# First tile's rows transposed at once, the second weight converted among the first products, the first expert's tiles taken as one, two, two, one

## The chip, the core and the metric

The kernel runs on one core of a Trainium2 chip. The metric is device microseconds (us) for one execution, from the first instruction to the end; the smaller the better. The core has five engines with queues of their own: TensorE (PE: products, and PEld: the loads of the stationary operand), VectorE (DVE), ScalarE (ACT), GpSimd (POOL) and SyncE (SP), which issues all DMAs here.

## The reference

Three stages stand one behind the other: attention with a block-causal mask (4 batches, 8 heads, 576 rows, 64 numbers a head), a layer of four experts, and a last layer with a softmax gate and a normalisation.

```python
scores = scale * np.matmul(q, k.transpose(0, 1, 3, 2))   # masked by blocks of 64
attn = softmax(scores); attn_out = np.matmul(attn, v)
x = attn_out.transpose(0, 2, 1, 3).reshape(B * S, H * D)  # 2304 x 512
p = domain_probs / (domain_probs.sum(-1, keepdims=True) + 1e-09)
for e in range(E):                                        # E = 4
    h = np.maximum(x @ w1[e], 0.0)                        # 512 -> 1024
    out += p[:, e:e + 1] * (h @ w2[e])                    # 1024 -> 512
# then: h = x @ w_in; solu = h * softmax(h); layer norm; @ w_out
```

## The kernel before

**Numbers as pairs.** A product of float32 values is made from three products of float16 pairs: a high part, and a low part that holds what the high part leaves. A weight is loaded in four parts as float32, its squares are summed on ACT (`square`, L127), a power-of-two scale is worked out (`scale`: L244, one product at L246, then DVE at L248, L131, L135 and L138), and each part is split (`split`: the high half on POOL at L257 or on ACT at L261, the low half on DVE at L264). For the first expert's two weights POOL makes the high halves. Queries and keys are prepared in the same manner (`parts`, L481 and L483, in most cases both on POOL), and so are values (`v_split`, L564 on POOL, L565 on DVE).

**Tiles and steps.** The 2304 rows are 18 tiles of 128. Tiles 0 and 1 hold the first 64 rows of two batches each; tiles 2 to 5 are the rest of the first batch. A tile takes several attention steps: two each for tiles 0 and 1, four for tiles 2, 3 and 4, eight for tile 5. So steps 0 to 3 are tiles 0 and 1, steps 4 to 7 tile 2 (scores 192 columns wide), 8 to 11 tile 3 (320 wide), 12 to 15 tile 4 (448 wide), and 16 onwards tile 5 (two halves of 288). A step has three parts: `step_a` makes scores (L600, L601, L604), `step_b` the exponentials (L639), their split (L643 on ACT, L644 on DVE) and a DMA transpose to `pT`, and `step_c` the products with the values (L673). When all steps of a tile are done, `finish` has three parts of its own: `rows` (L715) divides by the sums, `scale` squares the rows and works out a scale, `split` makes the pair (L726 on ACT, L727 on DVE) and transposes it by DMA to `xT`. From then on the experts can use the tile.

**Experts.** `emit_h` makes `h` of a run of k tiles: for each of 8 column blocks f of the first weight 12 products of 128*k columns (L306), and then one evacuation on ACT (L314) and one on DVE (L315) for every 3 // k column blocks. So a run of one tile takes the blocks as three, three and two; a run of two or three tiles takes one at a time. `emit_o` makes the second product of a tile, 24 products of 512 columns (L326). `h` lies in 8 buffers (`hp`); a run of two or three tiles uses all 8. The six tiles of the first part belong to expert 0 as six runs of one tile; all later phases have runs of three.

**The order.** The work up to step 3 is emitted from a string of letters (L958), one letter a piece: `a`, `b`, `c` are the three parts of the next step, `f` is the next of the three parts of `finish`, `W` the next piece of the first expert's first weight (its squares, scale and splits), `x` and `X` the same of its second weight (loads and pieces), `V` the next piece of the first batch's values (five squares, the scale, two splits), `N` the next keys and queries of tile 2, and `n, v, p, y, z, t, u` loads. Behind the string, what is left is emitted: for letters in a fixed order, then steps, then `finish`. All DMAs issued up to there keep their emitted order on SP (`InOrder`, L79).

Then a planner (L1009) emits the steps from 4 on and the expert units between them, by two clocks that it keeps itself. A unit waits until its last tile is `ready`. Pieces of weights come either from a list `bg` by step number, up to three behind a step, or as units among the expert units (`spread`, L978). In the kernel before, the rest of the first expert's second weight is in `bg` from step 2 on, and no expert unit is emitted before it is through (`len(bg) <= n1`, L1011).

The emitted order gives each instruction its rank. A scheduler then places instructions on each engine's queue, those that it thinks ready in the order of rank, so that ready work of a later rank can stand ahead of waiting work of an earlier one. Each engine runs its own queue in that order.

Of the kernel before, what the change touches and what calls it, by code (L numbers as in the profile page):

```python
# [58 lines left out]
def tile_kernel(  # L59
# [51 lines left out]
    psh = phs.enter_context(tc.tile_pool(name="psh", bufs=NPH, space=PSUM))  # L111
# [285 lines left out]
    def phase_units(j, runs, pool):  # L397

        e = j % E
        units = []  # L400
        for t0, k in runs:
            cost = 12 * (k * 128 / 2400 + 0.003)
            per = GT // k
            for f in range(0, KF, per):
                fs = range(f, min(f + per, KF))
                units.append((t0 + k - 1, lambda t=t0, k=k, fs=fs: emit_h(e, t, k, fs, pool), cost * len(fs)))
            for t in range(t0, t0 + k):
                units.append((
                    t, lambda t=t, o=(t - t0) * 128: out_unit(e, t, o, pool), 24 * 0.216,
                ))  # L410
        return units
# [474 lines left out]
    p1, q1 = next_w(gp, place_raw="w2")  # L886
# [44 lines left out]
    def token(c, left=0):  # L931

        for l in before.get(c, ""):
            while todo[l]:
                todo[l].pop(0)()
        if todo[c]:
            todo[c].pop(0)()
# [17 lines left out]

    ready = {}
    strict[0] = True
    for c in "naSyczZTPPnpwpWbcTZWzxufvWfWPpfzxSTfazSTPwTnbVbyWTapbnwabvvcVPNnVbnVPwxbNuXtPnztzu":  # L958
        if c == "f":
            at1.token_f()  # L960
        elif c in "abc":
            if c == "a" and at1.na < 20 or c == "b" and at1.nb < at1.na or c == "c" and at1.nc < at1.nb:
                getattr(at1, "token_" + c)()
        elif todo[c]:
            token(c)
# [10 lines left out]
    p1, q1 = todo["x"], todo["X"]  # L976

    def spread(units, *spans):  # L978

        todo = []  # L980
        for a, b, tasks in spans:
            todo += [(a + (b - a) * (k + 1) / len(tasks), fn) for k, fn in enumerate(tasks)]
        todo.sort(key=lambda x: x[0])
        res = []
        for j, u in enumerate(units):
            while todo and todo[0][0] <= j:
                res.append((None, todo.pop(0)[1], 0.0))
            res.append(u)
        return res + [(None, fn, 0.0) for _, fn in todo]


    p2, q2 = next_w()
    p3, q3 = next_w()
    bg = [(2, fn) for fn in p1 + q1]
    bg += [(14, fn) for fn in p2 + q2] + [(32, fn) for fn in p3]
    moe = phase_units(0, [(t, 1) for t in range(6)], psh)
    post = q3
    for j in range(1, 5):
        us = phase_units(j, GROUPS[j // E], psh)
# [5 lines left out]
    moe.reverse()  # L1005
    bg.reverse()
    tpe = tdv = 0.0
    n1 = len(p2 + q2 + p3)
    while at1.more:  # L1009
        t, u, cost = moe[-1] if moe else (-1, None, 0)  # L1010
        ok = t is None or t in ready and len(bg) <= n1  # L1011
        if not ok or tdv <= tpe + 2.0:
            at1.step()
            a, c = at1.cost()
            tdv, tpe = tdv + (a * 1.2 if at1.n < SLOW else PACE + c), tpe + c
            for _ in range(3):
                if bg and bg[-1][0] <= at1.n:
                    bg.pop()[1]()
        else:
            moe.pop()  # L1020
            u()
            tpe += cost
# [196 lines left out]
```

## Time and profile before

| what | value |
|---|---|
| median of 3 runs | 1137.04 us (1136.17 to 1137.23) |
| the profiled execution | 1137.2 us |
| its span, first to last instruction | 1135.4 us |
| TensorE products busy | 1072.7 us, 94% of the span |
| DVE, ACT, POOL busy | 712.2, 504.7, 181.6 us |
| mean granted TensorE clock | 0.991 of full speed |

The span lies 1.8 us under the execution's time. An engine is busy while an instruction of its own runs; products are pipelined, so a busy TensorE isn't one at its peak. The granted clock is the share of full speed (2.4 GHz) that TensorE had: 0.5 would be 1.2 GHz throughout.

### The profile page before, as it was taken

The numbers are of one execution on the slowest core, as the hardware profiler recorded it, in microseconds if no ns is written. First come the engines' busy times: TensorE is split into PE (matmuls) and PEld (weight loads), VectorE is DVE, ScalarE is ACT, GpSimd is POOL, SyncE is SP. The second block draws the span as 40 slices with busy tenths as digits, with TensorE's granted clock in tenths as the row PEclk, the third lists the DMA queues.
The fourth block names the chain that finished last, engine by engine and source line by source line (L and its number), as shares of the span: only waits on it lengthen the run. The fifth ranks groups of instructions, "written<-read, shape, count | busy, mean of one in ns | idle before, by whom it ended". The sixth has DMA issues, their size and how long they took to land.

```text
span 1135.4 us, 18547 instructions
## 1 busy us (share of the span) xinstructions
PE 1072.7 (94%) x7216; PEld 609.2 (54%) x7216; DVE 712.2 (63%) x1562; ACT 504.7 (44%) x1067; POOL 181.6 (16%) x176
## 2 busy tenths in 40 slices
PE   4579889899999999999999999999999999999998
PEld 4456766466556555655555555555555554444443
DVE  7988788557676876555313223232788646999883
ACT  5567676646656666562333213131324342333222
POOL 4975533224125310000000000000000000000000
PEclk9999999899999999999999999999999999999999
DMA  9768996738638747334121002020232111353343
GB/s 319 222 165 171 229 201 160 211 81 229 164 92 207 189 103 163 52 111 142 54 96 49 27 1 75 1 74 1 75 93 84 31 27 28 74 103 74 84 84 83
DMA packets 216056, 125.77 MB, mean 111 GB/s; under 512 B 183712, under 2 KB 185760, under 8 KB 215456
## 3 DMA queue, kind: packets, MB, share of 16 engines
q1 hardware_dynamic: 215968, 124.59, 42.7%
q8 instruction: 56, 0.92, 0.4%
q14 instruction: 32, 0.26, 0.1%
HBM read 73.18 MB, written 6.29 MB: 70 GB/s over the span
## 4 chain that ended last, share of the span: by engine, by line
PE 77%; DMA 8%; DVE 6%; POOL 4%; issue 2%; ACT 2%; SPq 1%; ACTq 0%; POOLq 0%; DVEq 0%
PE ops L326 29%; PE hps L306 27%; PE h L1070 8%; PE o L1133 8%; DMA pT<-hl 6%; PE pv L673 2%; DVE wt L264 1%; PE sps L600 1%; DMA stage<-in_w_dram 1%; DVE hl L644 1%; PE sps L601 1%; POOL wt L257 1%; POOL v L564 1%; ACT p L639 1%; POOL ks L483 1%
## 5 line engine op out<-in xcount | busy, mean ns | idle before, releaser
L306 PE MATMUL hps<-xT,wt 128*128 128x384 f16 (+1 forms) x2688 | 396.0, 305 | 3.5 <-DVE hch L315 3.1
L326 PE MATMUL ops<-wt,hch 128*128 128x512 f16 x1728 | 386.7, 381 | 2.5 <-DVE hch L315 1.3
L306 PEld LDWEIGHTS <-wt 128*128 128x128 f16 x2688 | 239.7, 99 | 138.4 <-issue 6.9
L326 PEld LDWEIGHTS <-hch 128*128 128x128 f16 x1728 | 167.4, 98 | 196.5 <-issue 6.0
L314 ACT ACTIVATE hch<-hps 128x384 f16<-128x384 f32 (+1 forms) x194 | 93.8, 485 | 232.1 <-PE hps L306 231.4
L315 DVE SCALAR_TENSOR_TENSOR hch<-hps,hch 128x384 f16<-128x384 f32 (+1 forms) x194 | 106.2, 550 | 131.1 <-ACT hch L314 130.7
L639 ACT ACTIVATE p<-sps,nm 128x320 f32<-128x320 f32 (+4 forms) x144 | 79.0, 552 | 80.8 <-DVE nm L610 46.6
L644 DVE TENSOR_TENSOR hl<-p,hl 128x320 f16<-128x320 f32 (+4 forms) x132 | 89.5, 692 | 33.7 <-ACT hl L643 33.3
L264 DVE SCALAR_TENSOR_TENSOR wt<-stage,ws,wt 128x1024 f16<-128x1024 f32 x72 | 97.4, 1377 | 12.8 <-ACT wt L261 11.5
L127 ACT ACTIVATE junk<-stage 128x1024 bf16<-128x1024 f32 x72 | 75.9, 1054 | 57.5 <-DMA stage<-in_w_dram 44.1
L350 DVE SCALAR_TENSOR_TENSOR acc<-ops,coef,acc 128x512 f32<-128x512 f32 x54 | 40.4, 748 | 90.8 <-PE ops L326 90.8
L1070 PE MATMUL h<-wt,x2T 128*128 128x512 f16 x432 | 95.5, 379 | 0.8 <-DVE acc L350 0.8
L1133 PE MATMUL o<-wt,lt 128*128 128x512 f16 x432 | 95.5, 379 | 0.0
L600 PE MATMUL sps<-ks,qhi 128*128 128x288 f32 (+3 forms) x160 | 66.0, 416 | 19.0 <-ACT p L639 8.4
L673 PE MATMUL pv<-v,pT 128*128 128x64 f16 x1392 | 56.2, 198 | 18.4 <-DMA pT<-hl 18.4
L261 ACT ACTIVATE wt<-stage,ws 128x1024 f16<-128x1024 f32 x64 | 70.4, 1141 | 4.6 <-DVE ws L138 4.6
L1070 PEld LDWEIGHTS <-x2T 128*128 128x128 f16 x432 | 42.2, 98 | 52.0 <-issue 1.1
L1133 PEld LDWEIGHTS <-lt 128*128 128x128 f16 x432 | 42.3, 98 | 51.0
L643 ACT ACTIVATE hl<-p 128x320 f16<-128x320 f32 (+4 forms) x132 | 66.0, 522 | 5.8 <-DMA pT<-hl 5.3
L673 PEld LDWEIGHTS <-pT 128*128 128x128 f16 x1392 | 50.6, 101 | 28.0 <-DMA pT<-hl 22.3
L1083 ACT ACTIVATE ex<-h,nb,cs 128x1024 f32<-128x1024 f32 x18 | 21.7, 1205 | 84.4 <-DVE nb L1080 43.6
L601 PE MATMUL sps<-ks,qlo 128*128 128x288 f32 (+3 forms) x160 | 51.5, 325 | 3.1 <-POOL qlo L483 3.1
(129 smaller groups left out, 951.6 us busy)
## 6 DMA issues: line engine op xcount, KB each, us to landing
stage<-in_w_dram SPq DMA_DIRECT2D x64, 512.0 KB, 5.6
raw<-in_qT_dram SPq DMA_DIRECT2D x34, 256.0 KB, 3.7
vraw<-in_vC_dram SPq DMA_DIRECT2D x30, 256.0 KB, 3.4
raw<-in_kT_dram SPq DMA_DIRECT2D x24, 288.0 KB, 3.5
raw<-in_w_in_dram SPq DMA_DIRECT2D x4, 1024.0 KB, 6.1
raw<-in_w_out_dram SPq DMA_DIRECT2D x4, 1024.0 KB, 4.9
out_dram<-o2s SPq DMA_DIRECT2D x16, 256.0 KB, 2.1
raw<-in_kT_dram SPq DMA_DIRECT2D x8, 192.0 KB, 4.3
```

Source lines behind the costliest of these rows:

```text
L127: return act.activation(out=junk, in_=x, func=AF.Square, accum_out=out)
L264: stage["last"] = vec.scalar_tensor_tensor(out=lo, in0=r, scalar=stage[key, "s"], in1=hi, op0=ALU.mult, op1=ALU.subtract)
L306: pe.matmul(ps[:, j * n:j * n + n], w[:, a, kk, f * 128:(f + 1) * 128], x[:, b * KD + kk, c0:c0 + n], start=(m == 0), stop=(m == 3 * KD - 1),)
L314: nc.scalar.activation(out=h[:, 0, :n], in_=ps[:, :n], func=AF.Relu)
L315: nc.vector.scalar_tensor_tensor(out=h[:, 1, :n], in0=ps[:, :n], scalar=0.0, in1=h[:, 0, :n], op0=ALU.max, op1=ALU.subtract)
L326: pe.matmul(ps, hch[f][:, a, o0:o0 + 128], w[:, b, f, :], start=(m == 0), stop=(m == 3 * KF - 1))
L600: pe.matmul(o, hi[:, h % 4], rhs, start=True, stop=False)
L639: act.activation(out=dst, in_=src, func=AF.Exp, bias=nm[:, j + x:j + x + 1], scale=SCALE, accum_out=sums[:, h:h + 1],)
L644: anc["D"] = vec.tensor_tensor(out=hl[:, W + c0:W + c0 + n_], in0=pf[:, 0:n_], in1=hl[:, c0:c0 + n_], op=ALU.subtract)
L673: pe.matmul(o, tt[:, a * nch + c, :], v[:, bb, hs], start=(m == 0), stop=(m == total - 1))
L1070: pe.matmul(ps[:, half], x[:, a * KD + kk, c:c + 128], w[:, b, kk, half * 512:half * 512 + 512], start=(m == 0), stop=(m == 3 * KD - 1),)
L1133: pe.matmul(ps, tt[:, a * KF + f], w[:, b, f], start=(m == 0), stop=(m == 3 * KF - 1))
```

## The change

Four edits, all to the first stretch of the kernel.

- The string of letters has another end. Behind the second of tile 0's value products (`c`), it now has: the three parts of tile 0's `finish`, the last six pieces of the first weight (a bookkeeping step, its place, four splits), both value products of tile 1, the three parts of tile 1's `finish`, and then values and tile 2's keys and queries, with one letter `X` among them, which issues the three missing loads of the second weight and its first square. Before, most of this was emitted by the loops behind the string, in another order.
- What is left of the second weight (three squares, the scale, its place and four splits, ten pieces with a bookkeeping step) no longer stands in `bg`. It is spread among the first three expert units: the squares before the second of them, the scale and the place before the third, the splits before the first second product.
- Expert 0 takes the six tiles as runs of one, two, two and one.
- The condition `len(bg) <= n1` is gone.

```diff
-    for c in "naSyczZTPPnpwpWbcTZWzxufvWfWPpfzxSTfazSTPwTnbVbyWTapbnwabvvcVPNnVbnVPwxbNuXtPnztzu":
+    for c in "naSyczZTPPnpwpWbcTZWzxufvWfWPpfzxSTfazSTPwTnbVbyWTapbnwabvvcfffWWWWWWccfffVVNVVVNXuVVVVNNNNN":
...
-    bg = [(2, fn) for fn in p1 + q1]
-    bg += [(14, fn) for fn in p2 + q2] + [(32, fn) for fn in p3]
-    moe = phase_units(0, [(t, 1) for t in range(6)], psh)
+    bg = [(14, fn) for fn in p2 + q2] + [(32, fn) for fn in p3]
+    moe = spread(phase_units(0, [(0, 1), (1, 2), (3, 2), (5, 1)], psh), (0.0, 2.9, p1 + q1))
...
-    n1 = len(p2 + q2 + p3)
     while at1.more:
         t, u, cost = moe[-1] if moe else (-1, None, 0)
-        ok = t is None or t in ready and len(bg) <= n1
+        ok = t is None or t in ready
```

The two strings are the same up to the letter behind `bvvc`.

## Rows read from the trace of the kernel before

**Rows 1.** Windows: stretch, length, busy us (count) per engine, granted clock, DMA.
```profile
30.40:50.90 20.50, 6.96 (x46) 5.77 (x47) 18.11 (x29) 13.04 (x37) 20.24 (x18) 1.00 0.80 215
58.00:76.70 18.70, 13.65 (x120) 8.20 (x118) 17.45 (x27) 10.73 (x32) 17.62 (x16) 0.91 0.52 132
76.70:82.00 5.30, 4.03 (x64) 3.42 (x65) 4.66 (x8) 3.47 (x9) 1.26 (x1) 1.00 1.09 224
82.00:102.80 20.80, 18.79 (x254) 14.17 (x251) 16.00 (x34) 17.01 (x41) 6.52 (x6) 1.00 0.95 192
480.00:1135.40 655.40, 650.93 (x3477) 332.14 (x3473) 363.63 (x834) 203.53 (x336) 0.00 (x0) 1.00 0.24 64
```
**Rows 2.** Timeline of DVE: tile 0's rows, their split, the second weight's scale.
```profile
30.42 0.69 DVE L715 TENSOR_TENSOR xf<-pv,ri 128x512 f32<-128x512 f32 x1
...
42.08 0.98 DVE L727 SCALAR_TENSOR_TENSOR xh<-xf,xs,xh 128x512 f16<-128x512 f32 x1
...
48.77 0.14 DVE L244 TENSOR_REDUCE wt<-wt 128x1 f32<-128x4 f32 x1
...
55.65 0.15 DVE L138 RECIPROCAL ws<-iw 128x1 f32<-128x1 f32 x1
```
**Rows 3.** Timeline of SP's queue: DMA issues; last, landing times of the xT transposes.
```profile
34.58 8.42 SPq L89 DMA_DIRECT2D stage<-in_w_dram  x5
...
43.09 1.24 SPq L89 DMA_TRANSPOSE xT<-xh  x1
...
79.00 1.24 SPq L89 DMA_TRANSPOSE xT<-xh  x1
...
DMA to landing us min/median/max: 2.7/4.2/5.6
```
**Rows 4.** Timeline of TensorE: start, length, line, what ended the idle time before.
```profile
50.96 2.35 PE L306 MATMUL hps<-xT,wt 128*128 128x128 f16 x24
...
60.13 0.42 PE L600 MATMUL sps<-ks,qhi 128*128 128x320 f32 x1 [1.71 <-POOL ks L483]
...
76.72 0.48 PE L600 MATMUL sps<-ks,qhi 128*128 128x448 f32 x1 [0.65 <-ACT p L639]
```
**Rows 5.** Timeline of POOL: splits of the second weight, and keys of tile 3.
```profile
56.08 1.46 POOL L257 TENSOR_SCALAR wt<-stage,ws 128x1024 f16<-128x1024 f32 x1
...
58.10 1.98 POOL L483 TENSOR_TENSOR ks<-raw,ks 64x384 fp32r<-64x384 f32 x1
...
60.66 1.73 POOL L257 TENSOR_SCALAR wt<-stage,ws 128x1024 f16<-128x1024 f32 x1
...
73.20 2.21 POOL L483 TENSOR_TENSOR ks<-raw,ks 64x384 fp32r<-64x384 f32 x2
```
**Rows 6.** L257 (POOL), then L264 (DVE): busy in windows; counts and ns min/median/max.
```profile
56.00:72.00 16.00, 5.76 (x4) 0.89 0.55 139
...
L257 POOL TENSOR_SCALAR wt<-stage,ws x8: 1112/1284/2076, 30.5 to 69.1; 128x1024 f16<-128x1024 f32 x8
...
L264 DVE SCALAR_TENSOR_TENSOR wt<-stage,ws,wt x8: 1274/1628/2282, 33.2 to 70.5; 128x1024 f16<-128x1024 f32 x8
```
**Rows 7.** L306 alone in windows: expert 0's first products, then 384 columns wide.
```profile
50.90:58.00 7.10, 6.67 (x96) 6.28 (x96) 1.00 0.78 227
66.00:76.70 10.70, 2.93 (x35) 2.19 (x35) 0.98 0.52 144
76.70:84.00 7.30, 3.73 (x61) 3.44 (x61) 1.00 1.05 222
94.00:103.00 9.00, 5.69 (x96) 5.46 (x96) 1.00 0.84 171
...
236.10:241.90 5.80, 5.73 (x36) 3.44 (x36) 1.00 0.58 140
```
**Rows 8.** L326 alone in windows: the second products of tile 0, then of tile 1.
```profile
60.00:76.70 16.70, 7.54 (x24) 2.54 (x24) 0.90 0.52 136
82.00:94.00 12.00, 5.67 (x24) 2.22 (x24) 1.00 1.03 207
```

## The prediction

> **What bounds the kernel now.** I read the page first: TensorE is busy for 94% of the span, no other engine for more than 63%. Then windows by stage [rows 1]. From 480 us to the end TensorE is busy for 650.9 of 655.4 us, so nothing the change does early can shorten the late part, and what it wins or loses early is handed on to the end in full: the time is TensorE's work plus its idle time, and the idle time lies in front. From 30.4 to 50.9 us TensorE is busy for 6.96 of 20.5 us, so 13.5 us are idle, while POOL is busy for 20.24 and DVE for 18.11 of them. From 58.0 to 76.7 it idles for 5.05, from 76.7 to 82.0 for 1.27, from 82.0 to 102.8 for 2.01 us [rows 1]. From 30 to 76 us, then, POOL and DVE set the pace.
>
> Next the timelines, for what TensorE could have done in those holes. Tile 0's rows are ready on DVE at 30.42 us, but their pair is made only at 42.08 [rows 2], transposed at 43.09 [rows 3], and the first expert product starts at 50.96 [rows 4]. That is the wait the change goes for. Behind it the steps of tile 3 wait for POOL: step 9's second half starts at 60.13, after 1.71 us of waiting for keys [rows 4], which stand on POOL's queue at 58.10 behind a split of the second weight at 56.08. The last keys of tile 3 are made at 73.20, behind four such splits [rows 5]. Tile 4's first scores, step 12, start at 76.72 [rows 4].
>
> **The change part by part.** I compare the point where TensorE is through with the same set of work: the steps up to 16, and for expert 0 tiles 0 and 1 (first and second products) and tile 2's first products. Before, that is at 102.8 us. After, tiles 1 and 2 share their first products, so the set is the same. Behind it the planner's order is nearly that of before, by its own clocks, so I carry the difference to the end.
>
> *Wider products.* Tiles 1 to 4 had 4 x 96 = 384 first products of 128 columns; they get 192 of 256. One of 128 columns takes 5.69/96 = 59.3 ns, one of 384 takes 5.73/36 = 159 ns [rows 7]; halfway is 109 for 256, which no row shows. Two of 59.3 less 109 is 9.6 ns, times 192 is 1.8 us. But the row of 128 columns is of several short runs between steps, each of which has its filling in it, while the wide one is a single run; a wide product takes no more than its columns at 2.4 GHz, and a third of 159 is 53. Were 128 columns 53 ns in a run of their own, nothing would be won. Bounds 0 and -1.8; I take -0.6, nearer to none, since the pair's runs will be cut by steps in the same manner.
>
> *Evacuations.* Runs of one tile have three pairs of ACT and DVE instructions, a run of two has eight: 18 before, 22 after. They lie beside products and cost TensorE nothing while two other banks are free; if DVE is full (17.45 of 18.7 us, [rows 1]) they would add some 0.5 us. I take 0.
>
> *Tile 0 earlier.* With its finishing parts in front of the four splits, its pair, 12.6 us behind the start of its rows [rows 2], should come in about half that, at 36 to 37 us (an estimate: the three DVE and ACT instructions on the way take under 1 us each), its transpose land (4.2 us, [rows 3]) near 42, and its 96 first products, 6.67 us [rows 7], fill the hole of 30.4 to 50.9. By itself this is worth nothing: the stretch that they leave, 50.9 to 58.0, has no other ready work, since step 9's second half waits for keys until 60.13 in any case. What is late next are POOL's keys. Pushed back in rank are tile 2's steps and keys; tile 1's finishing now goes ahead of steps 6 and 7, with 0.69 and 0.98 us on DVE as tile 0's had [rows 2]. Bounds 0 and +1.7; I take 0, as those steps wait for POOL too, which is busy for 20.24 of 20.5 us there [rows 1].
>
> *The second weight later.* Its last three loads were issued from 34.58 us on; SP keeps the emitted order, and there they now stand behind both transposes to xT, of which the first was at 43.09 [rows 3]. Its scale's chain, 48.77 to 55.65 us [rows 2], and its splits lose rank to tile 3's first queries and keys. POOL's four splits take 5.76 us [rows 6]; steps 9 and 10 had the first two, 1.46 and 1.73, in front of them [rows 5]. So tile 3's steps, and step 12 with them, come earlier by 0 (the scheduler keeps the old order), 3.2 (two splits pass behind) or 5.8 us (all four). I take -5.0, near the upper end, because loads and scale are both later.
>
> Here a rule speaks for more. A split on POOL took 1.11 us at least and 2.08 at most, one on DVE 1.27 and 2.28 [rows 6]; each is stretched where it lies beside the other. The Trainium skill, "SBUF — State Buffer", section "Who interferes with whom", says that a DVE instruction with two inputs in SBUF and a GpSimd one that reads SBUF exclude each other for the whole instruction. The trace agrees that they don't overlap freely. By that rule the moved DVE halves (at least 4 x 1.27 = 5.1 us) would leave POOL's way as well; were half of that on it, the -5.0 would be -7.5 and the time 1133.6, and the same would have to be paid later.
>
> *The pair waits for tile 2.* This is the price. Before, tile 1's 96 first products ran as 35 before step 12 (2.93 us) and 61 just behind it (3.73 us) [rows 7], filling holes up to 83. Now they need tile 2's xT, whose transpose was issued at 79.00 [rows 3], so some 83 us less whatever the steps gain. The fill lost is 2.93 + 3.73 = +6.7 us. Of this the idle 2.0 us between 82.0 and 102.8 can be won back, as the pair's work lies ready there: -2.0.
>
> *The clock.* Tile 0's 24 second products took 7.54 us at a granted clock of 0.91 over 58.0 to 76.7 [rows 1, 8]; tile 1's 24 took 5.67 at 1.00 [rows 8]. So TensorE ran part of that stretch at 1.2 GHz, and it cost 1.9 us. With less work between 50 and 75 this can repeat. Bounds -1.9 and +1.9; I take 0.
>
> *Sum.* -0.6 - 5.0 + 6.7 - 2.0 = -0.9 us, on the profiled 1137.2: 1136.3. The median lies 0.2 lower, which makes **1136.1 us**.
>
> **The rivals.**
>
> *Faster.* The second weight leaves POOL's way wholly (-5.8), and tile 2's rows come earlier by as much, at about 77 us, so that only the 35 products before step 12 are lost (+2.9), and 2.0 are won back: -0.6 - 5.8 + 2.9 - 2.0 = -5.5, 1131.5 us on the median's scale. For it: the chain of keys and splits on POOL sets steps 9 to 11 [rows 4, 5]. Against it: tile 0's second products then wait longer for the second weight.
>
> *Slower, by the pair.* The scheduler leaves the splits where they are among the keys, or DVE's first-weight work holds the steps back by as much. Then nothing comes off for the steps, the hole of 6.7 us stands with 2.0 won back, and TensorE falls to 1.2 GHz once more (+1.9): -0.6 + 6.7 - 2.0 + 1.9 = +6.0, 1143.0 us. It decides when step 12 comes less than about 2 us earlier than 76.72. For it: TensorE has nothing but steps and tile 0 until tile 2 is through.
>
> *Nothing moves.* The scheduler may place ready work of a later rank ahead of work that waits. If it draws the same work ahead as before, only the wider products are left: 1137.2 - 0.6 - 0.2 = 1136.4 us. Against it: tile 0's finishing was ready at 30.42 and still came late [rows 2], so rank did count there.
>
> **How the numbers follow.** The forecast has 0.38, with a range of its own of 1134.0 to 1138.5 from the 3.2 and 5.8 of the second weight; the faster case has 0.32, the slower 0.23, no move 0.07. A measurement of this kernel tells about 0.2%, 2.3 us, from no change. Of the forecast's 0.38, 0.06 lies below that and 0.03 above. So faster is 0.38, the same 0.36, slower 0.26. The range for 8 in 10 has to reach into both rivals: 1131.0 to 1142.0 us.
>
> **What would show it.** The step of tile 0: its first product starts before 45 us, and yet TensorE idles in the 50s. The second weight: the splits on POOL stand behind the keys of steps 9 and 10, and step 12's first score starts by 72.5 us. The pair: products of 256 columns, 192 of them, the first behind the third transpose to xT, and TensorE idle before it for 5 us or more. The refill: under 1 us idle from there until tile 1's second products. The prediction is wrong if step 12 is later than 75 us, if tile 2's rows land before 76 us, or if the idle time between 103 and 480 us, which I left as it is, changes by more than 3 us, since the scheduler's order there may shift too.

## The result and the profile after

The changed kernel took 1142.39 us (median; 1141.46 to 1146.81), 1.0054 of the time before, 95% interval 1.0038 to 1.0070: 0.5% slower, where I had forecast 1136.1 us, 0.1% faster, within 1131.0 to 1142.0. Its profiled execution took 1144.3 us with a span of 1142.5.

The windows of the changed kernel (stretch, length, busy us and count of PE, PEld, DVE, ACT and POOL, granted clock, DMA share, GB/s), cut as in [rows 1]:

```profile
30.40:50.90 20.50, 7.26 (x53) 6.27 (x54) 18.20 (x26) 9.39 (x30) 19.61 (x18) 1.00 0.46 113
58.00:76.70 18.70, 7.97 (x68) 6.85 (x68) 12.22 (x31) 11.63 (x29) 8.30 (x9) 0.56 0.80 212
76.70:82.00 5.30, 4.39 (x51) 2.82 (x49) 5.29 (x6) 5.30 (x17) 5.30 (x5) 0.93 0.80 195
82.00:102.80 20.80, 18.02 (x198) 13.45 (x196) 17.91 (x36) 14.43 (x40) 6.07 (x6) 1.00 0.65 149
480.00:1142.50 662.50, 658.04 (x3524) 336.83 (x3523) 368.05 (x843) 207.84 (x345) 0.00 (x0) 1.00 0.24 65
```

From 58.0 to 76.7 us TensorE is busy for 7.97 us, where it was 13.65 [rows 1], at a granted clock of 0.56 instead of 0.91; POOL, which set the pace there, is busy for 8.30 instead of 17.62. From 480 us on 4.46 us are idle, as before (4.47). The loss lies in front, and what was lost there was handed on to the end.

What POOL waited for is on SP's queue (start, us, operation):

```profile
43.35 1.24 SPq L89 DMA_TRANSPOSE xT<-xh  x1
...
62.69 1.24 SPq L89 DMA_TRANSPOSE xT<-xh  x1
63.98 1.59 SPq L89 DMA_DIRECT2D stage<-in_w_dram  x3
65.68 1.33 SPq L89 DMA_TRANSPOSE pT<-hl  x1
67.10 0.52 SPq L89 DMA_DIRECT2D raw<-in_kT_dram  x1
```

The three loads of the second weight start at 63.98 us, behind tile 1's transpose; before, they were part of the five at 34.58 [rows 3]. Behind them stand a step's transposed weights and the last keys of tile 3. The landing times of what was issued from 64 to 68 us (KB each, median us from issue to landing), first of the kernel before, then of the changed one:

```profile
raw<-in_kT_dram SPq DMA_DIRECT2D x1, 192.0 KB, 2.3
pT<-hl SPq DMA_TRANSPOSE x1, 3.1
```
```profile
stage<-in_w_dram SPq DMA_DIRECT2D x3, 512.0 KB, 5.2
...
raw<-in_kT_dram SPq DMA_DIRECT2D x1, 192.0 KB, 5.5
pT<-hl SPq DMA_TRANSPOSE x1, 6.5
```

Behind 1.5 MB the keys take 5.5 us instead of 2.3 and the weights 6.5 instead of 3.1. What that does on the engines, in the timelines of POOL, DVE and TensorE of the changed kernel:

```profile
72.80 0.51 POOL L481 TENSOR_SCALAR ks<-raw 128x384 fp32r<-128x384 f32 x1 [7.93 <-DMA raw<-in_kT_dram]
...
75.84 2.22 POOL L257 TENSOR_SCALAR wt<-stage,ws 128x1024 f16<-128x1024 f32 x2 [1.44 <-DVE ws L138]
```
```profile
30.11 0.68 DVE L715 TENSOR_TENSOR xf<-pv,ri 128x512 f32<-128x512 f32 x1
...
42.24 1.08 DVE L727 SCALAR_TENSOR_TENSOR xh<-xf,xs,xh 128x512 f16<-128x512 f32 x1
...
72.62 0.16 DVE L244 TENSOR_REDUCE wt<-wt 128x1 f32<-128x4 f32 x1 [5.99 <-ACT junk L127]
```
```profile
49.98 3.85 PE L306 MATMUL hps<-xT,wt 128*128 128x128 f16 x36
...
62.38 0.61 PE L600 MATMUL sps<-ks,qhi 128*128 128x320 f32 x1 [4.22 <-POOL ks L481]
...
72.21 0.82 PE L673 MATMUL pv<-v,pT 128*128 128x64 f16 x12 [4.57 <-DMA pT<-hl]
...
77.68 0.47 PE L600 MATMUL sps<-ks,qhi 128*128 128x448 f32 x1
...
85.59 1.46 PE L326 MATMUL ops<-wt,hch 128*128 128x512 f16 x6 [2.31 <-DVE wt L264]
...
89.66 3.00 PE L306 MATMUL hps<-xT,wt 128*128 128x256 f16 x26
```

Tile 0's pair is made at 42.24 us, as before (42.08, [rows 2]); TensorE's wait of 4.22 us in front of 62.38 ended before the three loads were issued, so it isn't theirs; POOL is idle for 7.93 us in front of the last keys; the second weight's scale begins at 72.62 instead of 48.77 [rows 2], its first split at 75.84 instead of 56.08 [rows 5]; step 12 starts at 77.68 instead of 76.72 [rows 4]; tile 0's second products end at 88.8 us, behind waits for the second weight; and the pair of tiles 1 and 2 starts at 89.66.

**An account of the time.** For every kernel below I cut the span into windows of 2 us (the first to 28 us, and the rest from 520 us, in one piece), and took from each the idle time of TensorE and, as lost to the clock, its busy time times what the granted clock lacks to 1. The rest of the busy time is work at full speed. The row of the kernel before: idle 62.7, lost 9.4, rest 1063.3, together its 1135.4. "Idle + lost" by stretch, in us:

| kernel | median, ratio to before | span of the profiled run | 0 to 58, idle | 58 to 102 | 102 to 200 | 200 to end | rest |
|---|---|---|---|---|---|---|---|
| before | 1137.04 | 1135.4 | 28.1 | 8.3 + 1.7 | 12.3 + 2.9 | 14.0 + 4.8 | 1063.3 |
| changed | 1.0054 | 1142.5 | 28.6 | 14.4 + 4.3 | 9.8 + 4.4 | 17.2 + 3.2 | 1060.6 |
| e1 changed, loads early | 1.0045 | 1143.5 | 28.8 | 10.0 + 6.9 | 10.2 + 4.3 | 17.2 + 5.5 | 1060.6 |
| e5 changed, runs of one | 1.0090 | 1143.5 | 28.4 | 12.1 + 3.0 | 9.2 + 3.3 | 18.9 + 5.5 | 1063.2 |
| e7 loads early, runs of one | 1.0021 | 1133.7 | 29.9 | 4.0 + 2.6 | 15.4 + 2.6 | 14.6 + 2.5 | 1062.1 |
| e10 loads between | 1.0112 | 1150.8 | 29.9 | 10.0 + 3.1 | 13.9 + 6.0 | 19.2 + 6.5 | 1062.2 |
| e12 loads behind keys | 1.0082 | 1145.2 | 29.0 | 9.1 + 6.8 | 13.4 + 4.3 | 16.9 + 2.8 | 1062.9 |
| e2 string only | 1.0093 | 1144.9 | 33.1 | 11.0 + 0.0 | 11.1 + 1.6 | 17.8 + 2.6 | 1067.7 |
| e8 string, loads early | 1.0030 | 1138.9 | 28.5 | 6.0 + 4.4 | 12.6 + 3.6 | 17.8 + 3.4 | 1062.7 |
| e3 spread only | 1.0012 | 1133.0 | 28.9 | 5.6 + 1.5 | 15.2 + 1.4 | 14.2 + 2.6 | 1063.5 |
| e4 runs only | 1.0024 | 1138.4 | 28.1 | 12.7 + 5.1 | 10.8 + 3.4 | 16.4 + 2.4 | 1059.5 |
| e6 spread and runs | 1.0026 | 1137.1 | 30.1 | 8.3 + 7.4 | 9.7 + 3.6 | 15.5 + 3.0 | 1059.6 |
| e11 late pair | 1.0048 | 1141.6 | 28.5 | 7.9 + 1.6 | 11.0 + 8.9 | 16.6 + 5.5 | 1061.5 |
| e13 late pair, filled | 0.9980 | 1135.7 | 28.4 | 8.7 + 0.0 | 11.0 + 8.1 | 10.5 + 1.6 | 1067.3 |
| e15 changed, filled | 1.0054 | 1146.3 | 28.9 | 14.5 + 7.3 | 10.6 + 4.5 | 12.7 + 1.6 | 1066.3 |
| e16 before, paced | 0.9982 | 1134.2 | 27.9 | 7.7 + 1.7 | 11.7 + 4.7 | 16.1 + 2.5 | 1062.0 |
| e17 changed, paced | 1.0047 | 1144.2 | 29.8 | 15.6 + 4.3 | 16.4 + 1.6 | 13.3 + 1.5 | 1061.7 |
| e18 spread, paced | 0.9959 | 1132.0 | 29.5 | 5.0 + 2.9 | 11.8 + 4.3 | 13.4 + 3.4 | 1061.7 |
| e19 late pair, paced | 0.9963 | 1130.2 | 28.6 | 8.4 + 0.0 | 13.1 + 6.1 | 10.8 + 0.0 | 1063.3 |

Of the changed kernel's 7.1 us more span, 8.7 came from 58 to 102 us (6.1 idle, 2.6 clock), 0.5 from before 58, 0.6 net from behind 102; the work at full speed was 2.7 less. One profiled execution isn't the median: those of e3 and e7 are the fastest of ten (1134.8 and 1135.5 us against medians of 1138.8 and 1139.3), that of e15 is the slowest of six (1148.2 against 1144.1). The ratios come from all executions, the stretches from the one that was profiled. One of e13's ten took 2013.7 us at a mean granted clock of 0.742, and its ratio is of the other nine.

### The profile page after: what moved, and what is told of

Read it like the earlier page. It is cut to its first block, busy times and chain, and to the rows that moved or that the text cites. A ratio compares the mean times of both kernels' runs of the same rounds, so it can differ in the third digit from the quotient of the medians.

```text
span 1142.5 us, 18160 instructions
## 1 busy us (share of the span) xinstructions
PE 1072.4 (94%) x7024; PEld 608.2 (53%) x7024; DVE 716.3 (63%) x1566; ACT 504.4 (44%) x1071; POOL 180.4 (16%) x176
## 4 chain that ended last, share of the span: by engine, by line
PE 78%; DVE 8%; DMA 7%; issue 3%; ACT 3%; SPq 1%; POOL 0%; DVEq 0%; ACTq 0%; POOLq 0%
PE hps L306 28%; PE ops L326 28%; PE h L1068 8%; PE o L1131 8%; DMA pT<-hl 3%; DVE wt L264 2%; PE pv L673 2%; PE sps L600 2%; DMA vraw<-in_vC_dram 1%; DMA stage<-in_w_dram 1%; DVE hl L644 1%; PE sps L601 1%; ACT p L639 1%; DVE v L565 1%; DVE nm L606 1%
## 5 line engine op out<-in xcount | busy, mean ns | idle before, releaser
L306 PE MATMUL hps<-xT,wt 128*128 128x384 f16 (+2 forms) x2496 | 397.5, 319 | 2.9 <-DVE hch L315 1.9
L326 PE MATMUL ops<-wt,hch 128*128 128x512 f16 x1728 | 383.8, 380 | 3.7 <-DVE wt L264 3.7
L306 PEld LDWEIGHTS <-wt 128*128 128x128 f16 x2496 | 238.4, 101 | 139.2 <-issue 5.5
L326 PEld LDWEIGHTS <-hch 128*128 128x128 f16 x1728 | 167.5, 98 | 198.0 <-issue 6.2
L264 DVE SCALAR_TENSOR_TENSOR wt<-stage,ws,wt 128x1024 f16<-128x1024 f32 x72 | 97.0, 1373 | 10.5 <-ACT wt L261 10.5
```

The source lines that it names most:

```text
L264: stage["last"] = vec.scalar_tensor_tensor(out=lo, in0=r, scalar=stage[key, "s"], in1=hi, op0=ALU.mult, op1=ALU.subtract)
L306: pe.matmul(ps[:, j * n:j * n + n], w[:, a, kk, f * 128:(f + 1) * 128], x[:, b * KD + kk, c0:c0 + n], start=(m == 0), stop=(m == 3 * KD - 1),)
L326: pe.matmul(ps, hch[f][:, a, o0:o0 + 128], w[:, b, f, :], start=(m == 0), stop=(m == 3 * KF - 1))
```

## The experiments: where the second weight's loads stand

**e1: the changed kernel with the loads early.** All string edits stand behind `...bnwabvv` in line 958.

```diff
-cfffWWWWWWccfffVVNVVVNXuVVVVNNNNN
+cxxxfffWWWWWWccfffVVNVVVNXuVVVVNNNNN
```

> The changed kernel with one edit: three letters x stand ahead of the three letters f, so that the second weight's last three loads are emitted before tile 0's finishing and stand on SP ahead of both transposes to xT. In the changed kernel they were issued at 63.98 us, behind tile 1's transpose at 62.69 (34.58 before), the sum of the squares came at 72.62 (48.77 before), and tile 0's last second products at 87.5 to 88.8 (72.8 to 74.0 before). Theory L, the loads' place on SP is the loss: the loads are issued before 45 us, the squares' sum lands before 60, tile 0's second products end before 78, the granted clock between 58 and 77 rises from 0.56 to over 0.8, and the time falls from 1142.4 to 1134 to 1138. Theory P, the pair that waits for tile 2 is the loss, as the prediction's slower case has it: the loads come early and yet step 12 and the pair start as late, and the time stays at 1141 or above.

Measured: 1143.6 us, 1.0045 [1.0025, 1.0065]. The loads started at 35.23 us, and tile 0's second products ran from 67 to 78 us instead of 77 to 89; yet no gain that can be told, as theory P had it and against theory L. The account shows why: 4.4 us less idle time between 58 and 102, 2.6 us more lost to the clock there, and 2.3 us more lost behind 200. The second weight's place is not all of the loss, and the pair's hole (below) stands in this kernel.

**e5: the changed kernel with runs of one.**

```diff
-spread(phase_units(0, [(0, 1), (1, 2), (3, 2), (5, 1)], psh), (0.0, 2.9, p1 + q1))
+spread(phase_units(0, [(t, 1) for t in range(6)], psh), (0.0, 2.9, p1 + q1))
```

> The changed kernel with one edit: expert 0 takes its six tiles as runs of one again. Theory L: the loads are as late as in the changed kernel (near 64 us), tile 0's second products end near 88, and the time stays above 1140; tile 1's first products now fill part of the hole before that, worth at most 5 us. Theory P: with tile 1's products back in the hole the time returns to 1135 to 1139.

Measured: 1147.52 us, 1.0090 [1.0065, 1.0116]: slower than with the pairs. So taking the pairs alone away doesn't win the time back; on top of the late loads they gave 0.36%, with intervals that touch. By the account e5 is better by 3.6 us from 58 to 102, where the pairs leave their hole, and worse by 4.0 behind 200 and by 2.6 in work at full speed.

**e7: runs of one and the loads early**, both edits above.

> The changed kernel with its three remaining loads of the second weight moved ahead of tile 0's transpose (as in the run with early loads) and, on top of it, expert 0's tiles as runs of one. Nothing is left of the change but the order of the string's end and the second weight's pieces among the expert units. Theory L (the loads' place on SP is the loss): with runs of one and late loads the kernel took 1.0090 of the time before; with early loads it should fall by 6 to 9 us, to 1.001 to 1.004. Theory P (the pair's wait for tile 2 is the loss): there is no pair, so 0.998 to 1.002, and the hole before tile 2's transpose (6 us of idle TensorE between 80 and 86 us) is gone. Theory S (the new end of the string itself, tile 1's finishing and the first weight's last splits ahead of steps 6 and 7, costs the time): still 1.006 or more.

Measured: 1139.32 us, 1.0021 [1.0004, 1.0038]. Against e5 only the loads moved, and 0.69%, 7.8 us, went. The windows from 58 us on, of e5 and then of e7:

```profile
58.00:76.70 18.70, 9.31 (x99) 8.08 (x100) 12.87 (x28) 12.36 (x32) 10.11 (x12) 0.63 0.86 229
```
```profile
58.00:76.70 18.70, 15.95 (x166) 12.54 (x167) 17.60 (x35) 15.42 (x42) 14.25 (x12) 0.82 0.64 165
```

TensorE is busy for 15.95 us instead of 9.31, at a higher clock. Of the two profiled executions' difference, 9.8 us, 8.5 lie from 58 to 102. Where no pair stands in the way, the place of three loads on SP is worth 0.7%.

**e2: the kernel before with the new string only; e8: the same with the loads early.**

```diff
-cVPNnVbnVPwxbNuXtPnztzu
+cfffWWWWWWccfffVVNVVVNXuVVVVNNNNN       (e2)
+cxxxfffWWWWWWccfffVVNVVVNXuVVVVNNNNN    (e8)
```

> The kernel before with the new string only: the planner's list with the second weight from step 2 on, its condition and the six runs of one stay. Theory L: the three loads stand behind both transposes to xT, and since no expert unit is emitted before the second weight is through, the loss is as in the changed kernel or larger: 1141 to 1146. Theory P: the string costs nothing without the pairs: 1135 to 1139.

> The kernel before with the new end of the string and with the three loads in front of tile 0's finishing parts; the second weight's pieces stay in the list by steps, the runs are of one. Against the run with the string alone (1.0093) only the loads move. Theory L: 0.999 to 1.003, no expert product waits until 76 us any more. Theory S: 1.006 or more, with the loads issued near 35 us and yet late first expert products, because the list by steps puts the second weight's pieces behind step 4 and the rest of the string.

Measured: e2 1148.11 us, 1.0093 [1.0076, 1.0110]; e8 1140.81 us, 1.0030 [1.0016, 1.0044]. Between them, too, only the loads differ: 0.63%. What the new string costs without them is 0.1 to 0.3% (e7 against e3 with its 1.0012, where the intervals overlap; e8 against before).

**e10: the loads between the transposes of tiles 0 and 1** (runs of one).

```diff
-cfffWWWWWWccfffVVNVVVNXuVVVVNNNNN
+cfffxxxWWWWWWccfffVVNVVVNXuVVVVNNNNN
```

> The changed kernel with runs of one, and the three loads of the second weight between the two transposes of tiles 0 and 1: on SP behind the first one (near 44.6 us), no longer behind the second (64 us). With the loads at 64 us runs of one took 1.0090 of the time before, with the loads at 35 us 1.0021. If any lateness of the loads costs in proportion, a third of the way: 1.0040 to 1.0055. If the loss is that of standing behind the second transpose, with the other loads and transposes behind them (theory L): 1.001 to 1.003.

Measured: 1150.49 us, 1.0112 [1.0091, 1.0133], the slowest of all and outside both expectations. The loads, started at 45.07 us, now stand ahead of the weights of the steps, and a score waited for its exponentials:

```profile
59.96 0.63 PE L600 MATMUL sps<-ks,qhi 128*128 128x320 f32 x1 [4.29 <-ACT p L639]
```

But the larger part of its loss lies behind 102 us (19.9 and 25.7 us idle and lost, against 18.0 and 17.1 in e7). Lateness in proportion is refuted, and so is that only the place behind the second transpose costs. That 1.5 MB in front of the steps' transfers cost at either place would fit both runs; e10 alone doesn't show it, since most of its loss lies elsewhere.

**e12: the loads behind the keys** (runs of one; `X` taken out of the string, the loads kept in order on SP).

```diff
-bg = [(14, fn) for fn in p2 + q2] + ...
-moe = spread(..., (0.0, 2.9, p1 + q1))
+bg = [(9, fn) for fn in p1] + [(14, fn) for fn in p2 + q2] + ...
+moe = spread(..., (1.0, 2.9, q1))
```

> The changed kernel with runs of one, and the three loads moved still later: behind the transpose of weights, the keys and the values that stood behind them on SP (so near 69 us instead of 64). Two theories on how the late loads cost 0.7% (1.0090 against 1.0021). Theory A, the second weight itself: its scale, splits and tile 0's second products come late; then 5 us later is worse, 1.0090 to 1.0130. Theory B, what stood behind the loads: tile 3's last keys and the transposed weights of its steps waited on SP and for the 1.5 MB; then they come early again, POOL no longer waits 7 to 8 us for keys, and the time is 1.002 to 1.006.

Measured: 1146.37 us, 1.0082 [1.0065, 1.0099], no different from e5, and outside theory B's range. B's mechanism was there: the loads started at 66.54 us, the keys landed 2.6 us after their issue again and POOL waited 2.01 us for them instead of 6.89. But the time didn't follow. The window of e12, and its step 12:

```profile
58.00:76.70 18.70, 10.91 (x71) 7.75 (x72) 15.45 (x31) 13.72 (x39) 10.11 (x11) 0.53 0.83 221
```
```profile
70.18 0.72 PE L600 MATMUL sps<-ks,qhi 128*128 128x448 f32 x1
```

The idle time fell (9.1 instead of 12.1 us from 58 to 102), and the loss to the clock rose by more (6.8 instead of 3.0). Step 12 started at 70.18 us, 6.5 us before the 76.72 of the kernel before, and the kernel was 0.8% slower all the same: tile 0's second products ended at 92.3 us instead of 87.4 in e5. That late loads cost by both parts, the second weight's own lateness and what stands behind it, would fit; it is argued, and how the cost divides stays open.

## The experiments: the pieces' place and the pairs

**e3: the second weight's pieces among the first expert units, nothing else** (old string, runs of one). This is the purest test of my step *The second weight later*.

```diff
-bg = [(2, fn) for fn in p1 + q1]
-bg += [(14, fn) for fn in p2 + q2] + [(32, fn) for fn in p3]
-moe = phase_units(0, [(t, 1) for t in range(6)], psh)
+bg = [(14, fn) for fn in p2 + q2] + [(32, fn) for fn in p3]
+moe = spread(phase_units(0, [(t, 1) for t in range(6)], psh), (0.0, 2.9, p1 + q1))
...
-        ok = t is None or t in ready and len(bg) <= n1
+        ok = t is None or t in ready
```

> The kernel before with the second weight's pieces among the first expert units and without the condition on the list; old string, runs of one. The old string issues the loads early (one X ahead of the values) so this measures the later splits alone. Theory L: the splits' rank costs nothing by itself, 0.998 to 1.002. My prediction's own step (the second weight later gives the steps of tile 3 and step 12 up to 5 us): step 12 starts by 72.5 us and the ratio is 0.996 to 0.999. Against both: tile 0's second products wait for the second weight and the ratio is 1.003 or more.

Measured: 1138.8 us, 1.0012 [0.9998, 1.0025]. The first split started at 64.89 us instead of 56.08 on POOL, behind the keys of steps 9 and 10 as I had said, and TensorE's idle time and lost clock from 58 to 102 fell by 2.9 us. POOL, then TensorE:

```profile
69.95 1.11 POOL L483 TENSOR_TENSOR ks<-raw,ks 64x384 fp32r<-64x384 f32 x1
```
```profile
79.64 0.47 PE L600 MATMUL sps<-ks,qhi 128*128 128x448 f32 x1 [0.61 <-ACT p L639]
```

The last keys of tile 3 were through at 71.06 us, 4.4 us before the 75.41 of the kernel before [rows 5]. But step 12 started at 79.64 us, later than 76.72, and 1.4 us more were idle and lost from 102 to 200. No gain is left in this order of the later work.

**e4: the runs one, two, two, one alone; e6: with the pieces' new place** (old string).

```diff
-moe = phase_units(0, [(t, 1) for t in range(6)], psh)
+moe = phase_units(0, [(0, 1), (1, 2), (3, 2), (5, 1)], psh)    (e4; in e6 within the spread of e3)
```

> The kernel before with one edit: expert 0 takes the six tiles as one, two, two, one; the string, the planner's list and its condition are those of before. Theory P: tile 1's 96 products (35 of them before 76.7 us, 61 behind) leave the stretch before tile 2's transpose at 79 us, some 5 us are lost and the time is 1140 to 1143. Theory L: the runs alone cost little, since the hole they make is filled behind tile 2: 1135 to 1139.

> The run before with expert 0's tiles as one, two, two, one: the change without the new end of the string. The runs alone took 1.0024 of the time before. If the costs add up, this is that ratio times the one of the pieces' place alone. Theory P: 1.002 to 1.004, with TensorE idle for 5 us or more before the third transpose to xT. Theory L: what the changed kernel lost comes from the string, so this is 2 us or more faster than the changed kernel, 1.000 to 1.003.

Measured: e4 1139.89 us, 1.0024 [1.0007, 1.0041]; e6 1140.59 us, 1.0026 [1.0013, 1.0039]. The hole is where the prediction put it. Two windows of e4 and two rows of TensorE:

```profile
76.70:82.00 5.30, 2.10 (x24) 1.42 (x23) 4.25 (x8) 4.05 (x13) 1.57 (x2) 0.80 1.16 189
82.00:102.80 20.80, 18.65 (x196) 14.92 (x197) 14.35 (x34) 12.54 (x36) 5.53 (x6) 0.81 0.77 161
```
```profile
80.24 1.14 PE L673 MATMUL pv<-v,pT 128*128 128x64 f16 x18 [2.58 <-DMA pT<-hl]
...
86.33 4.73 PE L306 MATMUL hps<-xT,wt 128*128 128x256 f16 x25 [1.30 <-DMA xT<-xh]
```

Step 12 is on time (76.44 us), TensorE is busy for 2.10 of 5.3 us instead of 4.03 [rows 1], and the pair starts at 86.33 at a clock of 0.81 where 1.00 was granted before: 4.4 us more idle and 3.4 us more lost from 58 to 102, against 3.8 us less work at full speed.

**e11: one pair only, tiles 3 and 4** (the kernel before with runs one, one, one, two, one).

```diff
-moe = phase_units(0, [(t, 1) for t in range(6)], psh)
+moe = phase_units(0, [(0, 1), (1, 1), (2, 1), (3, 2), (5, 1)], psh)
```

> The kernel before with expert 0's tiles as one, one, one, two, one: a single pair, tiles 3 and 4, and not the pair of tiles 1 and 2. The runs one, two, two, one took 1.0024 of the time before. Theory P (tile 1 waits for tile 2's rows while TensorE has nothing else): the early hole is gone, 0.999 to 1.0008. Rival: wider runs cost by themselves, by their evacuations or because all eight buffers of h are taken at once: half of the loss stays, 1.001 to 1.002.

Measured: 1142.47 us, 1.0048 [1.0033, 1.0063]. Both theories missed: the pair that I had thought harmless costs alone at least about as much as both pairs together (1.0048 against 1.0024, intervals overlapping). From 102 to 200 us it idles even less than the kernel before (11.0 against 12.3 us), but 8.9 us are lost to the clock instead of 2.9. Windows of e11:

```profile
111.00:114.00 3.00, 1.34 (x28) 1.19 (x29) 2.89 (x6) 0.97 (x3) 2.92 (x4) 1.00 0.83 294
114.00:117.00 3.00, 0.81 (x7) 0.72 (x5) 2.36 (x11) 3.00 (x8) 2.83 (x3) 0.52 1.11 345
117.00:120.00 3.00, 2.65 (x10) 2.17 (x10) 2.59 (x6) 3.00 (x7) 0.74 (x1) 0.50 1.08 261
...
126.00:129.00 3.00, 1.94 (x32) 1.95 (x32) 1.69 (x5) 2.11 (x6) 2.05 (x3) 0.50 1.08 242
```

In the kernel before 90 of tile 3's 96 first products ran from 109 to 120 us between the steps, and the clock stayed at 1.00 there. Without them TensorE was busy for 2.15 of 6 us, was granted 1.2 GHz from about 114 us, and stayed there beyond 129.

**e13: e11 with 96 products thrown away in front of the pair; e15: the changed kernel with 96 behind tile 0's first products.** They use the first weight and the tile's rows, in eight units of twelve, and are never read. `filler` makes the units; the cut shows e13's list, and e15's has them between tile 0's first and second products.

```diff
...
-phase_units(0, [(0, 1), (1, 1), (2, 1), (3, 2), (5, 1)], psh)
+phase_units(0, [(0, 1), (1, 1), (2, 1)], psh) + filler(3, psh) + phase_units(0, [(3, 2), (5, 1)], psh)
```

> The kernel before with the runs one, one, one, two, one (1.0048 of the time before) and, in front of the pair of tiles 3 and 4, 96 more products of tile 3's rows with the first weight, 128 columns each, whose results are thrown away. Without them TensorE idled for about as long as in the kernel before, but its granted clock fell to 0.83 and 0.72 between 103 and 140 us. Theory C (what the pair costs is the clock that falls in the hole it leaves): the added 5.7 us of products lie for 4 us in idle time, the clock stays at 1.00 there, and the time is 0.999 to 1.002. Rival (the wait itself costs): 1.005 to 1.010, the added products on top.

> The changed kernel with 96 more products of tile 0's rows with the first weight behind tile 0's own first products, thrown away. In the changed kernel TensorE idled for 10.7 of the 18.7 us from 58 to 76.7 at a granted clock of 0.56. Theory C: the added 5.7 us lie in that idle time, the clock is 0.8 or more there, and the time is 2 to 4 us less than the changed kernel's 1142.4, so 1.001 to 1.004. Rival (the second weight's late conversion and the pair's wait set the end of that stretch, whatever the clock): within 1.5 us of the changed kernel, 1.004 to 1.0065; and if the added products get into the steps' way, more.

Measured: e13 1136.74 us, 0.998 [0.9965, 0.9996], with 5.8 us more work at full speed than e11 (the account's last column); e15 1144.05 us, 1.0054 [1.0030, 1.0078]. e13 gave about the time that theory C forecast, but not by its way. Two windows of e13:

```profile
114.00:117.00 3.00, 2.96 (x46) 2.71 (x44) 2.15 (x6) 2.73 (x8) 2.83 (x3) 1.00 0.94 287
...
120.00:140.00 20.00, 15.94 (x171) 14.29 (x172) 13.55 (x24) 10.29 (x28) 10.96 (x12) 0.66 0.99 232
```

The clock held through the filled hole and fell behind it: 8.1 us are lost from 102 to 200, nearly as in e11. What was won, 10.0 us, lies behind 200 us, where no product was added. In e15 the products weren't placed in the hole at all (they ran from 76.58 us on), so it doesn't test theory C, and there too idle time and lost clock fell by 6.1 us behind 200. An added unit also moves the planner's clock, and with it every later step. So the next four kernels take the products away and leave the clock's shift.

**e16 to e19: eight empty units of 0.672 us on the planner's clock.** e16 is the kernel before, e17 the changed kernel (with the units behind tile 0's first products), e18 is e3, e19 is e11 (with them in front of the pair). The cut shows e16's list.

```diff
-phase_units(0, [(t, 1) for t in range(6)], psh)
+phase_units(0, [(t, 1) for t in range(3)], psh) + [(3, lambda: None, 0.672)] * 8 + phase_units(0, [(t, 1) for t in range(3, 6)], psh)
```

> The kernel before with eight empty units between the units of tiles 2 and 3: they emit nothing, but add 5.4 us to the planner's own clock of TensorE, as the thrown-away products did. The runs with those products did not win where the products lay (103 to 140 us), but behind 200 us: idle time and lost clock there fell from 18.8 us (before) to 12.1. Theory O (the planner's order of steps and expert units from there on is what won): 5 to 7 us less than before, 1130 to 1133, ratio 0.994 to 0.997. Theory C (the products kept TensorE's clock up): nothing is added here, so 0.999 to 1.001.

> The changed kernel with eight empty units behind tile 0's first products, 5.4 us on the planner's clock and no products. The same with products took as long as the changed kernel although it had 5.8 us more work. Theory O: the time falls by 4 to 7 us below the changed kernel's, 1135.5 to 1138.5, ratio 0.998 to 1.001, with the stretch of 58 to 103 us as bad as in the changed kernel. Theory C: no product, no gain, 1.004 to 1.006.

> The kernel before with the second weight's pieces among the first expert units (1.0012 of the time before, with idle time and lost clock between 58 and 102 us 3 us below before), and the eight empty units between tiles 2 and 3. Theory O: 4 to 7 us less than without the units, ratio 0.994 to 0.998. Theory C: 1.000 to 1.002.

> The kernel before with the runs one, one, one, two, one and eight empty units in front of the pair of tiles 3 and 4 (the run with thrown-away products there, without the products). Theory O: 4 to 6 us less than with the products, 1131 to 1134, ratio 0.993 to 0.997. Theory C: the hole is open again, as without the products, 1.003 to 1.006.

Measured: e16 1135.16 us, 0.9982 [0.9966, 0.9999]; e17 1143.22 us, 1.0047 [1.0024, 1.0071]; e18 1133.26 us, 0.9959 [0.9946, 0.9973]; e19 1133.14 us, 0.9963 [0.9949, 0.9977]. Nothing but the emitted order of steps and units was changed (TensorE, DVE, ACT and POOL have as many instructions as without the empty units), and e11 became 0.85% faster, e3 0.53%, the kernel before 0.18%, the changed kernel not measurably. So theory C is out as the reason of e13's gain: e19, with no product added, is faster still. Theory O holds for e18 and e19, fell short for e16 (2.7 us of the 5 to 7, by the medians) and failed for e17, where 5.6 us won behind 200 were lost again, 3.8 of them from 102 to 200 (18.0 against 14.2). e18 and e19 are faster than both kernels. e17 is 0.65% slower than e16, so the change's loss stands with empty units too, though they lie elsewhere in it. The stretch of e19 from 200 to 480 us, whose row of the kernel before has 270.42 us busy at 0.98:

```profile
200.00:480.00 280.00, 273.70 (x2186) 165.20 (x2185) 194.40 (x412) 175.98 (x401) 75.38 (x70) 1.00 0.61 153
```

## Why the prediction was wrong

**What bounds the kernel, and the carry to the end.** Right for this change: idle time behind 480 us stayed at 4.46 us, and from 102 us to the end idle time and lost clock rose by only 0.6 us net (34.0 to 34.6). As a rule it doesn't hold: over the other kernels the same sum runs from 29.4 (e15) to 45.6 us (e10). That the planner's order behind the edit stays nearly the same was an assumption that cost nothing here by luck.

**Tile 0 earlier.** The mechanism failed, its value of 0 held. The pair came at 42.24 us, not 36 to 37: two DVE splits of the first weight (3.68 us, from 32.84 us) still stood between the rows and their scale, and one (1.52 us, from 40.42) in front of the pair. An earlier pair could in any case not have started the first products before 41.9 us, where the first weight's last DVE split ended, since each sum of twelve products goes over all four blocks of that weight; they started at 49.98.

**The second weight later.** This is the step that failed. I saw that its three loads would stand behind both transposes to xT, and booked that only as a gain of 5.0 us for the steps. That tile 0's second products would wait longer I named under the faster rival and did not price, and what 1.5 MB on SP cost the transfers behind them I did not name: both stood at nothing in the sum. The Trainium skill, "DMA: Bandwidth & Descriptors", section "Queues, rings and completion order", says that on each DMA engine the descriptors of a queue are consumed in ring order; the trace agrees, with keys that landed in 5.5 us behind the loads and in 2.3 without them. Step 12 came 1.0 us later instead of 5.0 earlier; without these 5.0 us the sum would have stood at 1141.1 us. Moving the loads alone is worth 7.8 us with runs of one (e5, e7) and 7.2 with the old list (e2, e8); with the pairs it shows no gain (e1), of which more at the end of this section. And the gain itself isn't there as I derived it: in e3, with early loads, the splits moved behind the keys of steps 9 and 10, the last keys came 4.4 us earlier, step 12 came 2.9 us later, and nothing was won (+0.12%, interval from -0.02 to +0.25). Nor does an early step 12 carry to the end: in e12 it came 6.5 us earlier and the kernel was 0.8% slower. With the empty units the same pieces do win, 0.23% or 2.6 us (e18 against e16), so what they are worth hangs on the order behind them. No run tests the rule on shared ports, which I weighed for another 2.5 us.

**The pair waits for tile 2.** The mechanism is shown by e4 and the size was right: 6.7 - 2.0 = 4.7 us forecast, 4.4 us more idle time from 58 to 102. What was missing beside it is the clock.

**The clock.** I took 0 within 1.9 us either way. It cost 2.6 us more from 58 to 102 in the changed kernel, 3.4 in e4 and 5.7 in e6. In e4, e6 and e11 the clock fell behind the hole that the pair leaves, and the work that followed ran slower: a term that belongs to the pair's price, not beside it with an even chance of both signs. Late loads have it as well (5.1 us more in e12, without a pair).

**Wider products.** Forecast -0.6, bounds 0 and -1.8. In a run, 24 products of 256 columns took 2.78 us, 116 ns each, against 2 x 59.3 [rows 7]: 0.5 us over 192. The account has more, 1.6 to 3.8 us less work at full speed in the kernels with both pairs than in the kernel before (e15, with its added products, apart). The two don't agree, and I can't say which is nearer; other kernels with runs of one scatter from 1061.7 to 1063.5 there, e2 apart.

**The rivals.** *Slower, by the pair*, 1143.0 us at 0.23, came within a microsecond of the median, and its condition was met: step 12 wasn't 2 us earlier. It was right on the hole and on the clock. But its reason, that the splits stay among the keys, is not what happened, and in the changed kernel itself taking the pairs away won nothing (e5). That the number was right is luck, made of two errors: it left out the late loads, and it charged the pairs in full.

**What stays open.** The costs don't add up: late loads cost 0.7% with runs of one and 0.1% with the pairs (1.0054 against 1.0045, intervals overlap), pairs cost 0.24% on the old order and gave 0.36% on the late loads. From 58 to 102 us the account's rows (one profiled execution each) fit one reading: idle time and lost clock are 18.7 us in the changed kernel, 16.9 with the loads early (e1), 15.1 with runs of one (e5) and 6.6 with both (e7). By it tile 0's second products and tile 1's first products fill the same hole: with either of them late most of it stays, and only with both in time is it gone. The whole time, too, came down only with both (1.0021 in e7, against 1.0045 in e1 and 1.0090 in e5). That the pairs leave room for tile 0's second products is not borne out, since these ended at 87.4 us in e5 and at 88.8 in the changed kernel; what e5 lost lies behind 200 us and in its work. Why the order behind 102 us comes out better or worse in one kernel than in another was not settled; that it does, without any change of work, is shown by e16 to e19.

## What to carry to other kernels

A transfer that an edit moves is priced at both its ends: who waits for it, and who stands behind it on its queue, by its size; here three loads of 512 KB, moved past one wait, cost 0.6 to 0.7% where no pair stood in the way, more than any other part of the change. Where two parts of a change leave the same hole empty, taking back one of them can show nothing, so take back both as well. A hole in TensorE's work cost its idle time here and then, in most of these kernels, the slower clock of the work behind it, so price both together. Where a planner or scheduler re-orders everything behind an edit, measure the planner's own freedom first: eight empty units moved the time by up to 0.85%, more than the change did.

## What the runs showed of the hardware

The granted clock doesn't tell everything: a score of 320 columns took 0.61 us at 49.42 and 0.39 at 57.84 in the kernel before, and the clock was granted at 1.00 in both windows. I had read 1.00 as full speed; the account above does too, so its "rest" holds slow work as well, in front of 58 us and in places behind: in e2 TensorE idled for 9.49 us, and then a score of 448 columns took 0.72 us where step 12's took 0.48 in the kernel before [rows 4], at a granted 1.00. That would explain that e2 has no lost clock from 58 to 102 us and the largest "rest" of all. The kernel before, then e2:

```profile
49.42 0.61 PE L600 MATMUL sps<-ks,qhi 128*128 128x320 f32 x1
...
57.84 0.39 PE L600 MATMUL sps<-ks,qhi 128*128 128x320 f32 x1
```
```profile
72.87 0.63 PE L600 MATMUL sps<-ks,qhi 128*128 128x320 f32 x1 [9.49 <-POOL ks L483]
...
73.66 0.72 PE L600 MATMUL sps<-ks,qhi 128*128 128x448 f32 x1
```

At a granted 0.50 thirty products of 64 columns took 1.78 us (e11, 127.06 us), at 1.00 they took 1.05 (kernel before, 121.94 us): a factor of 1.7, so for such products "lost" in the account is rather too large. The spread of one kernel's executions goes with the clock as well: of e3's ten, the fastest (1134.8 us) had a mean granted clock of 0.994 and the slowest (1140.8) one of 0.985.
